# Four of six feature blocks of three batches transposed by DMA, in an mLSTM cell followed by a Fourier mix and an MLP

## The chip, the cores and the metric

The kernel runs on one core of one Trainium2 chip. The engines are TensorE (PE; its weight loads are PEld), VectorE (DVE), ScalarE (ACT), GpSimd (POOL) and SyncE (SP). SP computes nothing; it issues DMAs. The metric is the device time of one execution in microseconds (us). The runs shown before took 390.17, 390.27 and 390.72 us, with a median of 390.27.

## The reference

Two layers follow each other, over 4 batches, 8 heads, 768 tokens and head size 40 (so 320 features per token).

The first layer is an mLSTM cell: for each head a 40 x 40 state `C` and a vector `n` are carried over the tokens, with gates in a stabilised exponential form, and each token's output is `o * (C q) / max(|n q|, 1)`.

The second layer takes these outputs as `x` (4, 768, 320):

```
mixed = real(fft(fft(x, axis=tokens), axis=features))
u  = x + mixed
un = (u - mean(u)) / sqrt(var(u) + 1e-6)          # over the 320 features
out = u + max(un @ w_ch1, 0) @ w_ch2               # 320 -> 1280 -> 320
```

Everything is float32.

## The kernel before, in words

**Tiles.** A batch's 768 tokens are six chunks of 128 tokens. The mLSTM cell works chunk by chunk. The mix works on pairs of chunks, (0,5), (1,4) and (2,3), since the second of a pair is the mirror image of the first: one product over the features (`mix_feat`, L920) gives both chunks' mix in one PSUM bank `pu`. VectorE adds it to `x` (`mix_add`, L940: four additions and the statistics) and so makes `u` for one chunk. In this text one chunk's `u`, 128 tokens by 320 features, is called a feature block; there are six per batch, handled in the order `ORDER = (0, 5, 1, 4, 2, 3)`.

**From `u` to the MLP.** The MLP needs the features on the partitions, so each block is transposed. `mix_center` (L968) lets ACT subtract the mean and writes `uc`, 384 columns wide (320 features, 64 of them twice). `mix_turn` (L976) lets TensorE transpose it in three pieces of 128 x 128 into a PSUM bank `put`. `mix_turn_out` (L983) lets ACT copy that bank into `uT_bufs`. There are two `uT` buffers: the first holds blocks 0, 5 and 1, the second 4, 2 and 3; each is the moving operand of the MLP's first products (`mlp_in`, L1041, for the first batch; `mlp_block`, L1111, for the other three).

**The MLP.** For batches 1 to 3 both layers of the MLP are done with seven products in place of eight (a 2 x 2 block scheme). VectorE therefore forms sums: `weight_sums` and `out_weight_sums` once for the weights; `mlp_sums` (L1104) over the `uT` buffers at the beginning of a batch's MLP; `hidden_sums` (L1219) over the hidden layer, four sums S1 to S4 for each of three pairs of chunks. The second layer (`mlp_out_pair`, L1228) takes four steps per pair and adds its results to `u` by `residual` (L1186, the instruction is at L1190), and `store` (L1192) sends the chunk out. A PSUM bank of this layer is accumulated further after VectorE has read an intermediate value from it, so the next step of products waits for that reading.

**What sets the order.** All is written by hand. `at(slot, phase, fn, ...)` puts a call into a plan; `run` takes the plan in order of (slot, phase), and each engine gets its instructions in that order. Within a slot, the phases are EVAC (0), FILL (1), MAIN (2) and FILL_PE (3), with fractions between. A slot holds one step of the MLP in MAIN, and it is that which gives it its length, about 2.7 us where it is twenty products of 160 columns. The batches overlap: while batch b is in the second layer of its MLP, batch b+1 goes through its mix, and batch b+2 through its mLSTM cell. The MLP of batch b begins at slot `s_mlp` (31 + 32 b); its mix begins at `s_mix`, which is `s_mlp` - 9 for batch 1 and `s_mlp` - 12 for batches 2 and 3. `plan_batch` (L1312) holds the slots, counted from `s_mix`, of the three feature products (`feat`), of the six additions (`add`) and of the six centrings and transposes (`turn` and `late`).

**Queues.** All DMAs are issued by SP, in the order of the plan; a DMA that must wait holds up all behind it. SP's queue carries the loads of the mLSTM chunks (`mlstm_load`, `mlstm_load_max`, `mlstm_load_decay`, `mlstm_load_o`), moves of rows within SBUF (`halves_rows`) and the stores. ACT's queue carries the exponentials of the mLSTM chunks (L491) beside the centrings and copies.

**PSUM.** Four banks serve the mix and the MLP. Until batch 1 they are taken in the order of the string `turn` (L86), afterwards as the table `MIX` (L802) says.

The two buffers `hT_bufs` are used in batch 0 only.

Of the kernel before, what the change touches and what calls it, by code (L numbers as in the profile page):

```python
# [10 lines left out]
FP = mybir.dt.float32  # L11
BF = mybir.dt.bfloat16
I32 = mybir.dt.int32
U32 = mybir.dt.uint32
AF = mybir.ActivationFunctionType
# [4 lines left out]
L = 128  # L20
# [24 lines left out]
M_INIT = -1.0e30  # L45

# [7 lines left out]
def kernel(  # L54
# [31 lines left out]
    turn = iter("3210321032120312031230123012012301023130201320132013203120123021320321")  # L86
# [21 lines left out]
    uT_bufs = [const.tile([L, 3, TG, L], FP, name=f"uT{n}") for n in range(2)]  # L108
# [10 lines left out]
    G_d = dram.tile([NT, BH, L], FP, name="G_d")  # L119

# [641 lines left out]
    def plan_halves(b, s0, stride=3):  # L762
        for c in range(NT):
            s = s0 + stride * c
            t = 22 + 2 * c if b == 1 and c < 3 else s - 5
            at(t, FILL, mlstm_load, b, c)
# [13 lines left out]
            if (b, c) == (3, 2):  # L780
                at(s + 2, MAIN + 0.1, halves_weigh, b, c)
            else:
                at(s + 1, FILL + 0.55 if b == 1 and c > 0 else MAIN + 0.7, halves_weigh, b, c)
# [6 lines left out]
            at(s + (5 if (b, c) == (2, 2) else 4), {(2, 4): FILL + 0.3, (3, 3): FILL - 0.3}.get((b, c), FILL + 0.3 if b == 1 else MAIN + 0.55), mlstm_finish, b, c)  # L790
# [11 lines left out]
    MIX = {"z": (2, 3), "zt": 2, "u": (3, 2, 2), "ut": (3, 3, 3, 3, 2, 3)}  # L802
# [172 lines left out]

    def mix_turn(b, c):  # L976

        k = mixes[b]
        pt = k.pt[c] = bank("put", [L, 3, L], MIX["ut"][ORDER.index(c)] if b > 1 else None)
        for ch in range(3):  # L980
            nc.tensor.transpose(pt[:, ch, :], k.uc[c].rearrange("p two n -> p (two n)")[:, ch * L:(ch + 1) * L], ident)  # L981

    def mix_turn_out(b, c):  # L983
        k = mixes[b]
        n = ORDER.index(c)
        nc.scalar.copy(out=uT_bufs[n // TG][:, :, n % TG, :], in_=k.pt[c])  # L986
# [23 lines left out]
    def plan_mix(b, s0, x_done, s_feat, s_add, s_turn):  # L1010
        for j in range(TG):
            p = TG - 1 - j
            at(x_done[j] + (b > 1 and j == TG - 1), FILL + 0.5 if b < 2 else FILL_PE + 0.2, mix_fold, b, p)
            if b == 0:
                at((s0 - 4, s0 - 2, s0)[j], FILL_PE + 4, mix_seq, b, p, (0, 1))
                at((s0 - 2, s0 - 2, s0)[j], FILL_PE + 4, mix_tail, b, p)
            elif b == 1 or j == 0:
                if b > 1:
                    for step, slot in enumerate((x_done[0], x_done[-1] + 2, x_done[-1] + 6)):
                        at(slot, FILL_PE + 0.25, mix_fold_again, b, step)  # L1020
                at(s0, FILL_PE + 4, mix_seq, b, p, (0,))
                at(s0 + 1, FILL_PE + 4, mix_seq, b, p, (1,))
                at(s0 + 2, FILL_PE + 4, mix_tail, b, p)
        for i in range(2):
            at(s0 + 1 if b == 0 else s0 + 1 + i, FILL, mix_seq_out, b, i)
        at(s0 + (1 if b == 0 else 3), FILL + 0.1, mix_tail_out, b)
        for p in range(TG):
            at(s_feat[p], FILL_PE + 4, mix_feat, b, p)
        for c, a, t in zip(ORDER, s_add, s_turn):
            at(a, FILL if b < 2 else MAIN - 0.3 if c == 0 else MAIN + 0.5, mix_add, b, c)  # L1030
            at(t, FILL + 0.1, mix_center, b, c)
# [9 lines left out]
    def mlp_in(b, gr, f):  # L1041
# [3 lines left out]
        u = [uT_bufs[gr][:, ch].rearrange("p c t -> p (c t)") for ch in range(3)]  # L1045
# [55 lines left out]
    def mlp_u(gr, ch):  # L1101
        return uT_bufs[gr][:, ch].rearrange("p c t -> p (c t)")

    def mlp_sums(n0, n1):  # L1104

        T2, T3, T4 = w1x["T"]
# [164 lines left out]
    def plan_mlp(b, s):  # L1271
# [20 lines left out]
        for n in range(TG) if b > 0 else ():  # L1292
            for step in range(4):
                at(s, MAIN, mlp_out_pair, b, n, step)
                if n < TG - 1 and step > 1:
                    for j in (2 * step - 3, 2 * step - 2):
                        at(s, MAIN + 0.6, hidden_sums, n + 1, (j,))
# [14 lines left out]
    def plan_batch(b, s_mlstm, s_mix, s_mlp):  # L1312
# [9 lines left out]
        else:  # L1322
            feat = [s_mix + c for c in ((3, 4, 6) if b == 1 else (3, 4, 7))]
            add = [s_mix + c for c in ((4, 4, 5, 6, 7, 7), (4, 5, 5, 6, 8, 9), (4, 4, 5, 6, 8, 9))[b - 1]]
            turn = [s_mix + c for c in ((5, 6, 6) if b == 1 else (6, 7, 8))]
            late = [s_mix + c for c in ((7, 8, 8) if b == 1 else (9, 10, 10))]
# [165 lines left out]
```

## Time and profile before

| | before |
|---|---|
| median of the runs | 390.27 us (390.17 to 390.72) |
| profiled execution, its own time | 390.34 us |
| span of its trace | 388.6 us |
| granted TensorE clock | 1.00 |
| TensorE busy | 378.2 us, 97% |
| VectorE busy | 276.2 us, 71% |
| ACT busy | 172.4 us, 44% |
| POOL busy | 136.7 us, 35% |
| transposes of the mix (L981) | 72 |
| copies from `put` (L986) | 24, 477 ns each |
| centrings (L974) | 24, 613 ns each |

How to read it: the busy time of TensorE counts an instruction from its start to its modelled end, and neighbouring products overlap, so that the distance from one start to the next is shorter than the duration shown. In a list of waits, "A <- B: 0.6, 2, 0.3" says that A waited for B 0.6 us in total, twice, 0.3 us at the longest. In the chain that ended last, each row is a start, a length, and the engine and line that the end of the program is traced back to.

The mix and the change of batch from the trace, where the first product of the MLP starts: batch 1 at 161.6 us, batch 2 at 246.6 us, batch 3 at 324.0 us.

### The profile page before, as it was taken

Reading aid. Unit: us, or ns where it says so; the run is one execution under the profiler, and the core shown is the slowest. Engines: PE = TensorE matmul, PEld = TensorE weight load, DVE = VectorE, ACT = ScalarE, POOL = GpSimd, SP = SyncE. Lnnn points to the kernel's source line nnn. Section 1 sums busy time; section 2 is a strip of 40 time slices with the busy share of each in tenths; the row PEclk is TensorE's granted clock in tenths of the full one; section 3 lists DMA queues with packets and bytes.
Section 4 is the critical chain, followed back from the end, with each engine's and each line's share of the span. In section 5 each row is a group of like instructions: output and inputs, shape, how many; then the busy total and the mean of one; then the engine's idle time right before and its main releaser. Section 6 shows DMA issues by size and latency. Waiting matters only on the chain.

```text
span 388.6 us, 10587 instructions
## 1 busy us (share of the span) xinstructions
PE 378.2 (97%) x4174; PEld 276.4 (71%) x4174; DVE 276.2 (71%) x671; ACT 172.4 (44%) x481; POOL 136.7 (35%) x237
## 2 busy tenths in 40 slices
PE   8999899999999999999999999999999999999996
PEld 6887455556567677665579989755588995556996
DVE  8699987599698687576975699767655785246652
ACT  6996367377352124564462315454530133545000
POOL 5787415277955433172354133541500000020000
PEclk9999999999999999999999999999999999999999
DMA  7969499678494435538601636400000000000101
GB/s 213 313 195 306 134 236 249 185 217 232 143 229 131 126 98 156 147 87 221 143 11 36 156 101 185 126 19 2 0 2 34 18 19 34 2 0 0 35 34 35
DMA packets 25631, 44.78 MB, mean 115 GB/s; under 512 B 5727, under 2 KB 14766, under 8 KB 25454
## 3 DMA queue, kind: packets, MB, share of 16 engines
q1 hardware_dynamic: 25582, 44.11, 40.8%
q8 instruction: 33, 0.54, 0.6%
q14 instruction: 16, 0.13, 0.1%
HBM read 38.49 MB, written 4.12 MB: 110 GB/s over the span
## 4 chain that ended last, share of the span: by engine, by line
PE 79%; DVE 11%; ACT 4%; DMA 2%; issue 2%; POOL 1%; DVEq 0%; ACTq 0%; POOLq 0%
PE po L1240 20%; PE pm L1121 15%; PE po L1184 8%; PE pm L1059 7%; PE ph L519 4%; PE pm L1126 4%; PE pu L938 4%; PE ps L519 3%; DMA so<-in_o 2%; PE pm L1050 2%; PE put L981 2%; PE pz L907 1%; PE pz L895 1%; DVE h L1130 1%; PE pi L139 1%
## 5 line engine op out<-in xcount | busy, mean ns | idle before, releaser
L1190 DVE SCALAR_TENSOR_TENSOR x<-po,rstd,x 128x160 f32<-128x160 f32 (+1 forms) x69 | 27.1, 394 | 37.7 <-PE po L1240 32.5
L1130 DVE TENSOR_TENSOR h<-h,pm 128x384 f32<-128x384 f32 x60 | 30.5, 549 | 27.1 <-PE pm L1121 12.4
L652 POOL TENSOR_TENSOR C<-C,decB 128x164 f32<-128x164 f32 x30 | 15.9, 529 | 67.9 <-DVE C L667 43.2
L1121 PE MATMUL pm<-uT,w_sb 128*128 128x384 f32 x90 | 37.7, 506 | 1.3 <-DVE uT L1109 0.6
L491 ACT ACTIVATE W<-W,colT 128x64 f32<-128x64 f32 x144 | 37.5, 339 | 1.0 <-DMA W<-M_d 1.0
L1184 PE MATMUL po<-w_sb,h 128*128 128x320 f32 x120 | 34.2, 435 | 0.0
L1005 POOL TENSOR_TENSOR t<-rstd 128x6 f32<-128x6 f32 x12 | 3.3, 272 | 79.9 <-DVE v L999 79.4
L515 POOL TENSOR_SCALAR_AFFINE_SELECT W<-W 64x512 f32<-64x512 f32 x36 | 27.3, 758 | 10.8 <-ACT W L491 5.3
L1059 PE MATMUL pm<-uT,w_sb 128*128 128x384 f32 x80 | 29.2, 500 | 0.1
L1184 PEld LDWEIGHTS po<-w_sb,h 128*128 128x128 f32 x120 | 22.3, 190 | 9.5 <-issue 0.6
L501 POOL TENSOR_TENSOR qg<-qk,Gb 128x512 f32<-128x512 f32 (+1 forms) x21 | 27.1, 1292 | 2.8 <-DMA Gb<-G_d 2.8
L1240 PE MATMUL po<-T,S 128*128 128x160 f32 x180 | 27.8, 301 | 0.3 <-DVE x L1190 0.3
L1240 PEld LDWEIGHTS po<-T,S 128*128 128x128 f32 x180 | 25.5, 190 | 1.7 <-DVE x L1190 0.5
L1121 PEld LDWEIGHTS pm<-uT,w_sb 128*128 128x128 f32 x90 | 15.5, 189 | 15.6 <-DVE h L1130 6.7
L1240 PE MATMUL po<-w_sb,h 128*128 128x160 f32 x180 | 26.3, 300 | 0.0
L1240 PEld LDWEIGHTS po<-w_sb,h 128*128 128x128 f32 x180 | 25.2, 190 | 1.4 <-DVE x L1190 0.3
L986 ACT COPY uT<-put 128x384 f32<-128x384 f32 x24 | 11.2, 477 | 30.1 <-PE put L981 30.1
L507 POOL TENSOR_TENSOR vw<-kvt,colT 128x328 f32<-128x328 f32 x23 | 19.9, 863 | 12.7 <-DMA qk<-in_qkT 10.1
L1177 ACT ACTIVATE h<-h 128x384 f32<-128x384 f32 x45 | 23.1, 520 | 2.0 <-DVE h L1130 2.0
L1126 PE MATMUL pm<-uT,w1t_sb 64*128 64x384 f32 x120 | 23.4, 508 | 0.0
L1059 PEld LDWEIGHTS pm<-uT,w_sb 128*128 128x128 f32 x80 | 14.1, 189 | 9.6 <-issue 1.9
L974 ACT ACTIVATE uc<-x 128x384 f32<-128x384 f32 x24 | 14.4, 613 | 12.6 <-DVE x L966 11.1
(241 smaller groups left out, 841.5 us busy)
## 6 DMA issues: line engine op xcount, KB each, us to landing
kvt<-in_kv SPq DMA_DIRECT2D x24, 336.0 KB
qk<-in_qkT SPq DMA_DIRECT2D x48, 160.0 KB
raw<-in_w SPq DMA_DIRECT2D x10, 640.0 KB
Gb<-G_d SPq DMA_DIRECT2D x36, 128.0 KB
W<-M_d SPq DMA_DIRECT2D x36, 128.0 KB
so<-in_o SPq DMA_DIRECT2D x24, 160.0 KB
out<-x SPq DMA_DIRECT2D x24, 160.0 KB
x<-so SPq DMA_DIRECT2D x9, 140.0 KB
```

What stands on the lines that cost most here:

```text
L491: nc.scalar.activation(out=k.W[:, h, :], in_=M, func=AF.Exp, scale=-1.0, bias=colT[:, c, 0, b * H + h:b * H + h + 1])
L501: nc.gpsimd.tensor_tensor(out=k.qg[:, :, t], in0=k.qk[:, 0, :, t], in1=k.Gb[:, :, t], op=OP.mult)
L515: nc.gpsimd.affine_select(out=W, in_=W, compare_op=OP.is_ge, fill=0.0, base=base, pattern=[[0, H], [step, LH]], channel_multiplier=-1)
L519: nc.tensor.matmul(out, w, x, start=start, stop=True, skip_group_check=True)
L1059: nc.tensor.matmul(k.pm[i], w1_sb[:, ch, f0:f0 + L], u[2 * ch], start=(ch == 0 and not ahead), stop=(ch == 1 and ahead), skip_group_check= ...
L1121: nc.tensor.matmul(bank, w, u, start=start, stop=True, skip_group_check=True)
L1126: nc.tensor.matmul(bank, block(w1t_sb, i)[rows], mlp_u(gr, 1)[rows], start=False, stop=True, skip_group_check=True)
L1130: nc.vector.tensor_tensor(out=h, in0=h, in1=bank, op=OP.add)
L1177: nc.scalar.activation(out=h, in_=h, func=AF.Relu, scale=-1.0)
L1184: nc.tensor.matmul(k.po[gr, i], hidden(gr, f)[:, i * L:(i + 1) * L], w2_sb[:, f, :], start=(f == 0), stop=(f == NFF - 1))
L1190: nc.vector.scalar_tensor_tensor(out=u, in0=po, scalar=k.rstd[:, c:c + 1], in1=u, op0=OP.mult, op1=OP.add)
L1240: nc.tensor.matmul(po, a[:, f], w[:, f], start=start and f == 0, stop=f == half - 1, skip_group_check=True)
```

## The change

For batches 1, 2 and 3, the first four blocks in `ORDER` (0, 5, 1 and 4; `TURNED = 4`) no longer go through TensorE, the PSUM bank `put` and the copy by ACT. After the centring, `mix_words` lets ACT copy the block as halfwords: each float32 of `uc` is two words of 16 bits, and the copy puts the 384 first words of a token and then its 384 second words into one of the buffers `hT_bufs`. ACT itself issues a DMA that writes this to a scratch tensor in HBM, 256 rows (token and word) of 384 halfwords. `mix_words_turn` lets SP issue a transposing DMA from there into `uT`, where the 256 halfwords of a feature are again 128 float32 values. Blocks 2 and 3, and all of batch 0, are transposed as before.

The layout of `uT` changes with it, from (3, chunk, 128) to (chunk, 3, 128): a block is now one contiguous piece, and the MLP reads three pieces of 128 columns.

Around this, places in the plan change: the second product over the tokens and the tail of batches 2 and 3 one slot earlier; the feature products and additions of the first four blocks one slot earlier in part, some centrings too; in batch 2's stretch (the MLP of batch 1) S3 and S4 of the last pair later or at another phase; three placements of the mLSTM chunks of batch 3 (`halves_weigh` of chunk 1, `mlstm_finish` of chunk 0, and the load of chunk 5 two slots earlier); the PSUM banks of the third feature product.

```diff
-    turn = iter("3210321032120312031230123012012301023130201320132013203120123021320321")
+    turn = iter("321032103212031203123012301201230102313020132013201320312012302130")
...
-    uT_bufs = [const.tile([L, 3, TG, L], FP, name=f"uT{n}") for n in range(2)]
+    uT_bufs = [const.tile([L, TG, 3, L], FP, name=f"uT{n}") for n in range(2)]
...
+    uc_d = dram.tile([B - 1, TURNED, 2 * L, 3 * L], U16, name="uc_d")
...
-            at(t, FILL, mlstm_load, b, c)
+            at(*((t - 2, FILL + 0.95) if (b, c) == (3, 5) else (t, FILL)), mlstm_load, b, c)
...
+            elif (b, c) == (3, 1):
+                at(s + 2, MAIN + 0.4, halves_weigh, b, c)
...
-    MIX = {"z": (2, 3), "zt": 2, "u": (3, 2, 2), "ut": (3, 3, 3, 3, 2, 3)}
+    MIX = {"z": (2, 3), "zt": 2, "u": (3, 2, 3), "ut": (3, 3, 3, 3, 2, 3)}
...
+    def mix_words(b, c):
+        k = mixes[b]
+        n = ORDER.index(c)
+        words = hT_bufs[n % 2].rearrange("p n t -> p (n t)").bitcast(U16)[:, 0:6 * L].rearrange("p (w m) -> p w m", w=2)
+        of = k.uc[c].rearrange("p two n -> p (two n)").bitcast(U16).rearrange("p (n w) -> p w n", w=2)
+        nc.scalar.copy(out=words, in_=of)
+        nc.scalar.dma_start(out=uc_d[b - 1, n].rearrange("(t w) m -> t w m", w=2), in_=words)
+
+    def mix_words_turn(b, c):
+        n = ORDER.index(c)
+        nc.sync.dma_start_transpose(out=uT_bufs[n // TG][:, n % TG].bitcast(U16), in_=uc_d[b - 1, n])
...
-        nc.scalar.copy(out=uT_bufs[n // TG][:, :, n % TG, :], in_=k.pt[c])
+        nc.scalar.copy(out=uT_bufs[n // TG][:, n % TG], in_=k.pt[c])
...
-                at(s0 + 1, FILL_PE + 4, mix_seq, b, p, (1,))
-                at(s0 + 2, FILL_PE + 4, mix_tail, b, p)
+                at(s0 + (b == 1), FILL_PE + 4, mix_seq, b, p, (1,))
+                at(s0 + (2 if b == 1 else 1), FILL_PE + 4, mix_tail, b, p)
...
+            if b > 0 and c in ORDER[:TURNED]:
+                at(t, FILL + 0.1, mix_center, b, c)
+                at(t, FILL + 0.11, mix_words, b, c)
+                at(*{(1, 1): (t, FILL + 0.95), (1, 4): (t, FILL + 0.95), (2, 5): (t + 1, FILL + 0.95),
+                     (2, 1): (t + 2, FILL - 0.7), (2, 4): (t + 1, FILL - 0.7)}.get((b, c), (t + 1, FILL - 0.55)),
+                   mix_words_turn, b, c)
+                continue
...
-        return uT_bufs[gr][:, ch].rearrange("p c t -> p (c t)")
+        return uT_bufs[gr][:, :, ch]
...
-                        at(s, MAIN + 0.6, hidden_sums, n + 1, (j,))
+                        at(*((s, MAIN + 0.6) if b != 1 or n == 0 or j < 3 else (s + j - 3, MAIN + 0.2)), hidden_sums, n + 1, (j,))
...
-            feat = [s_mix + c for c in ((3, 4, 6) if b == 1 else (3, 4, 7))]
-            add = [s_mix + c for c in ((4, 4, 5, 6, 7, 7), (4, 5, 5, 6, 8, 9), (4, 4, 5, 6, 8, 9))[b - 1]]
-            turn = [s_mix + c for c in ((5, 6, 6) if b == 1 else (6, 7, 8))]
-            late = [s_mix + c for c in ((7, 8, 8) if b == 1 else (9, 10, 10))]
+            feat = [s_mix + c for c in ((3, 4, 5) if b == 1 else (2, 3, 7))]
+            add = [s_mix + c for c in ((4, 4, 5, 5, 6, 6), (3, 4, 5, 6, 8, 9), (3, 4, 5, 6, 8, 9))[b - 1]]
+            turn = [s_mix + c for c in ((5, 5, 6) if b == 1 else (5, 6, 7))]
+            late = [s_mix + c for c in ((6, 7, 8) if b == 1 else (8, 10, 10))]
```

## The prediction

> **What bounds the kernel.** The page first: the span, TensorE's share of it, and the chain that ended last.
>
> ```profile
> span 388.6 us, 10587 instructions
> PE 378.2 (97%) x4174; PEld 276.4 (71%) x4174; DVE 276.2 (71%) x671; ACT 172.4 (44%) x481; POOL 136.7 (35%) x237
> ...
> PE 79%; DVE 11%; ACT 4%; DMA 2%; issue 2%; POOL 1%; DVEq 0%; ACTq 0%; POOLq 0%
> ```
>
> TensorE is busy for 97% of the span, so what leaves its queue shortens the kernel, unless something makes it wait. Next, TensorE's waits from 120 to 330 us, the stretch that holds all three changed stages:
>
> ```profile
> PE pm L1121 <- DVE uT L1109: 0.6, 2, 0.3
> PE pm L1121 <- DVE h L1130: 0.5, 2, 0.3
> PE po L1240 <- DVE x L1190: 0.3, 1, 0.3
> PE ph L519 <- ACT warm L699: 0.3, 1, 0.3
> ```
>
> Total, count, longest: 1.7 us of waiting in 210 us. Are the transposes in that queue paid in full? Their group (all 72), then TensorE's timeline in batch 3 (start, length):
>
> ```profile
> L981 PE MATMUL put<-ident,uc x72: 272/273/332, 54.0 to 322.5; 128*128 128x128 f32 x72
> ```
>
> ```profile
> 312.83 2.88 PE L1240 MATMUL po<-w_sb,h 128*128 128x160 f32 x20
> 315.55 0.49 PE L981 MATMUL put<-ident,uc 128*128 128x128 f32 x3
> 315.88 1.52 PE L1240 MATMUL po<-T,S 128*128 128x160 f32 x10
> 317.24 1.52 PE L1240 MATMUL po<-w_sb,S 128*128 128x160 f32 x10
> ```
>
> One transpose lasts 273 ns, but they overlap: what counts is from the first start to the next product's, 315.88 - 315.55 = 0.33 us for a block's three. Last, the chain in batch 2, where it leaves TensorE:
>
> ```profile
> 224.72 0.39 DVE x L1190
> 225.10 0.23 DVE x L960
> ...
> 235.35 0.73 DVE s_last L1226
> 236.08 0.24 DVE C L667
> 236.32 0.30 DVE x L1190
> 236.62 0.04 issue
> 236.67 0.40 PE po L1240
> ```
>
> From 224.7 to 236.6 VectorE works without a gap of its own, and TensorE's product at 236.67 waits for a residual that stands at the end of this backlog. In batch 2, then, VectorE is as tight as TensorE; in batches 1 and 3 it has holes.
>
> **The skill.** (1) "DMA: Bandwidth & Descriptors", section DMA Transpose (X-bar): it transposes two-byte elements only, is issued from SP or ACT, and must write to SBUF. Hence float32 is split into two halfwords. No run before shows one. (2) The same page, Latency and other measured facts: 261 GB/s in one kernel, 350 to 400 for a contiguous one; not in this trace. (3) "VectorE: DVE Perf Modes", The three transpose paths: 1309 ns for one 128x128 two-byte tile through DMA, 390 ns on TensorE; the trace has 273 ns (float32) and 0.11 us of queue. (4) "ScalarE: Activation LUTs", What ACT_TABLE_LOAD costs: an activation with immediate scale takes 186 ns + 0.833 ns per element. That gives 506 ns for 384 elements; the trace has 477 for L986, so it agrees roughly.
>
> **The change, part by part.**
>
> *Removed from TensorE:* four blocks in each of three batches, three transposes each. 12 x 0.33 = 3.96 us. Some intervals are longer (0.38 at 229.21, 0.39 at 232.77), but those follow small products, and the cold start passes to whatever comes next, so I take 0.33. From ACT go 12 copies of 477 ns.
>
> *Added to ACT, per block:* a copy of 768 halfwords, read at a stride of two. Estimate by (4): 186 + 640 = 826 ns; if the stride costs double, 1.5 us. Then one DMA issue; ACT issues none before, and SP's for a store take 349 ns. Net 0.83 + 0.35 - 0.48 = 0.7 us per block, 8.4 us in all (up to 16). ACT has 13.8 of 38.9 us busy from 122.8 to 161.7, 17.3 of 46.8 in batch 2, 8.4 of 39.2 in batch 3: its idle time covers this. Behind it in ACT's queue stand the exponentials of the next chunk; their masks and weighing come a slot or more (2.7 us) later. Without that cover it would be up to 1.4 us per slot.
>
> *Added to DMA, per block:* 196 KB written to HBM and read back turned. The last store is issued at 385.9 and the span ends at 388.6, so at most 2.7 us for 160 KB; I take 2.5 for the write. The transposing read: at best as a plain DMA, 2.5 us; at worst six 128x128 tiles of 1.31 us one after another, 7.9 us. I take 3.
>
> *Is it in time?* Batch 1 is tightest. Its adds and centres run in slots 58 to 60; ACT gets blocks 1 and 4 at about 147.9 (before's clock), needs per block 0.62 + 0.83 + 0.35 = 1.8, and has issued block 4's write at 151.5. It lands at 154, is turned by 157. TensorE wants it when the MLP begins: 161.7 - 1.3 = 160.4, with sums (L1109) just after. Slack 3.4 us. In batch 2 blocks 1 and 4 are turned in slot 92, from about 237 to 240.5, due at 246.6 less three or four blocks and the wait, 244.8: slack about 4. In batch 3 block 4's copy is done at about 314, written by 316.5, turned by 319.5, due at 324.0 - 1.3 = 322.7: slack 3.
>
> *SP's queue:* each transpose waits for its write, and everything behind it waits too. Between them in batch 1 stand the loads of chunk (2,4), used four slots later; in batch 2, the loads of (3,4) and (3,5), the latter placed two slots earlier, ahead of the waits. Stores need no haste. The loads wait up to 2 to 4 us more and are used at least 8 us later: nothing. If that cover went, POOL's query scaling would start late and products from chunks wait, some 2 us once.
>
> *Moved products* (second sequence product, tail, features, one slot earlier): the same instructions, at no cost. The tail's copy (0.48) still lies under the 2.72 us of ten-plus-ten products between it and the features. New PSUM banks for the third feature block: its old content is added two slots before.
>
> *VectorE in batch 2:* the add of block 5 (1.75 us, 224.99 to 226.76 in the trace) leaves the backlog for a slot with holes of 1.1 us, and S4 (0.73) goes behind the residual. That residual comes 2.5 us earlier, TensorE only three blocks (1.0 us) earlier, so the wait of 0.30 and the cold start after it (2.98 against 2.72) go: 0.5 us. The waits at 249.9 and 255.0 follow from VectorE's sums at 247.8 to 254, whose order does not change: 0.
>
> *uT read in three pieces:* TensorE reads it as 3 x 128 columns with gaps, in 360 instructions. An operand read at a stride of two costs no more than a contiguous one (L895: two of 193 columns from 203.97 to 204.31, 0.34 us; L904: 122.02 to 122.35, 0.33), so I take 0; the upper end is the difference, 5 ns on each, 1.8 us.
>
> **Sum** against the profiled execution's 390.34 (span 388.6 and 1.7 around it): 390.34 - 3.96 - 0.5 = 385.9. The median of the runs is 390.27, 0.07 less: 385.8.
>
> **Rivals.**
>
> *The transposes are slow (slower than before).* If one holds the crossbar for T and they run in series, batch 1's four start at about 146.8, when SP has issued the row moves that it begins at 144.65 (2.10 us), and end at 146.8 + 4T, against 160.4. Beyond T = 3.4 TensorE stands still at the start of the MLP, where nothing else is in its queue. With T = 4.5 batch 1 loses 4.4 us, all of the gain: there it decides. With T = 5: 6.4 in batch 1, and in batch 2 two transposes from 237 to 247 against 244.8, 2.2 more: 385.8 + 8.6 = 394.4. At 7.9: 18, 8 and about 2, some 414. For it: four are issued nearly together, and the price per tile in (3). Against: that price is for one tile alone, with its latency; the rates in (2) move 196 KB in 0.5 to 0.75 us.
>
> *VectorE keeps batch 2 (less gain).* If the backlog of 224.7 to 236.6 only moves, batch 2's 1.3 and 0.5 are lost, or ACT's and SP's added work brings as much waiting anywhere: 387.6. For it: VectorE's closed chain. Against: the holes of 1.1 us in the slots to which the add goes.
>
> *More gain.* VectorE, relieved, also begins the sums of batch 2 earlier, and the 0.6 us of waits there and the lost starts behind them go: 384.6. Against: they hang on a residual that TensorE itself releases at 244.75.
>
> *No change:* the transposes were hidden anyway, or waits take exactly their time. Against: each product starts right after them, with no idle time shown.
>
> **Chances.** Forecast 0.60, its own range 385.1 to 386.8; less gain 0.15 (386.8 to 389.4); more gain 0.06 (384.5 to 385.1); no change 0.04; slow transposes 0.15. A measurement here tells about 0.2% (0.8 us) from nothing, so faster 0.81, same 0.04, slower 0.15. The three gaining cases hold 0.81: the range is 384.5 to 389.4, whose upper end also takes in 1.8 us for the three pieces and more.
>
> **What would show it.** 36 transposes on TensorE in place of 72, at the same 273 ns; TensorE's busy time down by some 4 us and its waits before the first product of each MLP under 0.5 us. ACT with 12 new copies near 0.83 us. On SP, transposes whose waits are under 4 us; no late loads in POOL's waits. In batch 2 no wait of TensorE for L1190. I am wrong if TensorE waits for uT (L1109 or L1121) by microseconds, if the copies take over 1.5 us and the exponentials come late, or if products from uT get slower than the 0.341 us of 14 in 4.78.

## The result, and the profile after

| | before | after |
|---|---|---|
| median of the runs made together | 390.74 us | 387.6 us |
| ratio after / before, 95% interval | | 0.9922 [0.9906, 0.9938] |
| profiled execution | 390.34 us | 387.23 us |
| its span | 388.6 us | 385.4 us |
| TensorE busy | 378.2 us | 374.8 us |

The kernel became faster by 0.78%, some 3.0 us. The forecast was 4.5 us. Measured again (experiment 5) the ratio was 0.9932 [0.9916, 0.9948]. Both intervals lie above the ratio that the forecast implies, 385.8 / 390.27 = 0.9885: the direction and the main mechanism were right, about 1.4 us of the gain did not come. The median of 387.6 us lies in the range that the forecast gave to "less gain" (386.8 to 389.4, chance 0.15) and not in its own (385.1 to 386.8, chance 0.60).

The page of the changed kernel: span, busy times, the DMA queues that carry most and that carry instructions (packets, MB, share of 16 engines), and the chain.

```profile
span 385.4 us, 10538 instructions
PE 374.8 (97%) x4138; PEld 273.4 (71%) x4138; DVE 277.5 (72%) x671; ACT 177.5 (46%) x481; POOL 138.0 (36%) x237
...
q1 hardware_dynamic: 35182, 46.47, 45.0%
...
q8 instruction: 32, 0.52, 0.6%
...
PE 82%; DVE 9%; ACT 3%; DMA 2%; issue 2%; POOL 1%; DVEq 0%; SPq 0%; POOLq 0%; ACTq 0%
```

TensorE still bounds the kernel at 97% of a shorter span; its share of the chain rose from 79 to 82%. The parts of the change, by their tiles (count, then shortest, median and longest duration in ns):

```profile
L998 PE MATMUL put<-ident,uc x36: 272/273/330, 54.1 to 319.3; 128*128 128x128 f32 x36
L986 ACT COPY h<-uc x12: 815/832/833, 143.6 to 309.7; 128x768 uint16<-128x768 uint16 x12
L987 ACTq DMA_DIRECT2D uc_d<-h x12: 338/338/577, 144.4 to 310.5; - x12
L991 SPq DMA_TRANSPOSE uT<-uc_d x12: 1209/1240/2201, 147.0 to 313.5; - x12
```

Half of the 72 transposes are left on TensorE. The copy of 768 halfwords takes 832 ns, where the estimate was 826. The issue of a transposing DMA holds SP for 1.24 us; I had counted SP's time only as waiting. Now TensorE's waits from 120 to 330 us (total, count, longest), as before shown for the kernel before:

```profile
PE ph L522 <- issue: 0.9, 1, 0.9
PE put L998 <- ACT uc L979: 0.4, 1, 0.4
PE po L1264 <- DVE x L1214: 0.3, 1, 0.3
PE pm L1145 <- DVE uT L1133: 0.2, 1, 0.2
PE ph L522 <- ACT warm L702: 0.2, 1, 0.2
PE pm L1145 <- DVE h L1154: 0.2, 1, 0.2
```

Three of these are new, and they are where the missing gain must be looked for first: a stop of 0.9 us at products from a chunk that waited for nothing the profile shows, a transpose (`put`) that waits for its centring, and a product that waits for a residual at a new place. TensorE's timeline says where (start, length, and in brackets the idle time before it):

```profile
221.02 1.63 PE L1264 MATMUL po<-T,S 128*128 128x160 f32 x10 [0.34 <-DVE x L1214]
248.47 0.44 PE L522 MATMUL ph<-kvt,W 64*64 64x41 f32 x16 [0.92 <-issue]
319.07 0.55 PE L998 MATMUL put<-ident,uc 128*128 128x128 f32 x3 [0.39 <-ACT uc L979]
```

The same timeline, read from start to start of TensorE's instructions, gives the length of each stretch. "Mix" runs from the first sequence product of batch 1, or from the first product of the previous MLP's second layer, to the first product of this batch's MLP; "first layer" from there to the second layer; the last column ends where the last run of ten products starts.

| us | mix 1 | first layer 1 | mix 2 | first layer 2 | mix 3 | MLP 3 to last products |
|---|---|---|---|---|---|---|
| before | 39.61 | 38.01 | 46.93 | 38.09 | 39.33 | 59.93 |
| after | 38.39 | 37.77 | 46.08 | 38.04 | 38.33 | 59.92 |
| difference | -1.22 | -0.24 | -0.85 | -0.05 | -1.00 | -0.01 |
| forecast | -1.32 | 0 | -1.82 | 0 | -1.32 | 0 |

The differences add up to -3.37 us; with 0.18 us of a later start they make the -3.19 us by which the last products start earlier. The forecast's terms add up to -4.46 us. So 1.1 us is missing in this pair of traces: 0.97 in batch 2, 0.32 in batch 3 and 0.10 in batch 1, less 0.30 gained where nothing was forecast.

### The profile page after: what moved, and what is told of

Read it like the earlier page. It is cut to its first block, busy times and chain, and to the rows that moved or that the text cites. A ratio compares the mean times of both kernels' runs of the same rounds, so it can differ in the third digit from the quotient of the medians.

```text
span 385.4 us, 10538 instructions
## 1 busy us (share of the span) xinstructions
PE 374.8 (97%) x4138; PEld 273.4 (71%) x4138; DVE 277.5 (72%) x671; ACT 177.5 (46%) x481; POOL 138.0 (36%) x237
## 4 chain that ended last, share of the span: by engine, by line
PE 82%; DVE 9%; ACT 3%; DMA 2%; issue 2%; POOL 1%; DVEq 0%; SPq 0%; POOLq 0%; ACTq 0%
PE po L1264 21%; PE pm L1145 16%; PE po L1208 9%; PE pm L1083 7%; PE ph L522 5%; PE pm L1150 4%; PE pu L943 4%; PE ps L522 4%; DMA so<-in_o 2%; PE pm L1074 2%; PE pz L912 1%; PE pz L900 1%; PE put L998 1%; DVE h L1154 1%; PE pi L142 1%
## 5 line engine op out<-in xcount | busy, mean ns | idle before, releaser
L494 ACT ACTIVATE W<-W,colT 128x64 f32<-128x64 f32 x144 | 37.4, 338 | 1.3 <-ACT h L986 0.5
L1250 DVE TENSOR_TENSOR S<-h,h 128x640 f32<-128x640 f32 (+2 forms) x24 | 17.1, 710 | 3.5 <-ACT h L1201 3.5
```

What stands on the lines that cost most here:

```text
L494: nc.scalar.activation(out=k.W[:, h, :], in_=M, func=AF.Exp, scale=-1.0, bias=colT[:, c, 0, b * H + h:b * H + h + 1])
```

## The experiments

Twelve kernels ran. Ratios are to the kernel before on the same chip. Each kernel has one trace. In six traces of kernels that are the same up to the MLP of batch 2, mix 2 lies between 46.08 and 46.95 us; the table of the changed kernel above is the lowest of them.

**1. Without the route.** The transposes of the four blocks are gone and nothing takes their place: no copy to halfwords, no write, no transposing read, so that `uT` holds old values in these blocks.

```diff
-                at(t, FILL + 0.11, mix_words, b, c)
-                at(*{(1, 1): (t, FILL + 0.95), ...}.get((b, c), (t + 1, FILL - 0.55)), mix_words_turn, b, c)
```

> The changed kernel without the copy into halfwords, the write to HBM and the transposing DMA of blocks 0, 5, 1 and 4; the MLP of batches 1 to 3 then reads what lies in uT from earlier (this part of the computation is left out). Theory A: the whole DMA route lies beside other work, and the 1.3 us that the forecast is short of comes from waits for VectorE and ACT in batches 2 and 3. Then this kernel takes as long as the changed one, 387.2 to 387.7 us, with the same waits of TensorE: 0.3 us for a residual near 221 us, 0.4 us for a centring near 319 us. Theory B: the route costs something (SP's queue, DMA traffic, ACT's longer queue, a stop of instructions such as the 0.92 us near 247.5). Then this kernel is 0.8 to 1.3 us faster, 386.0 to 386.6, and the 0.92 us stop is gone.

Measured: 386.93 against 391.26 us, ratio 0.9889 [0.9871, 0.9908], span 385.2. The removal together with the new plan is worth 4.3 us. The interval, 3.6 to 5.0 us, holds the forecast's 4.46 and also the 3.96 of the transposes alone. Its stretches: 38.38, 37.65, 45.80, 38.10, 38.39, 59.93; they add up to 3.65 us less than before. TensorE's waits in the same window:

```profile
PE pm L1141 <- DVE uT L1129: 0.6, 2, 0.3
PE pm L1141 <- DVE h L1150: 0.5, 2, 0.3
PE put L998 <- ACT uc L979: 0.4, 1, 0.4
PE po L1260 <- DVE x L1210: 0.3, 1, 0.3
PE ph L522 <- ACT warm L702: 0.3, 1, 0.3
```

The waits for the residual (0.34 us at 220.98) and for the centring stay without the route: they belong to the rearranged plan. The stop named "issue" is gone: that belongs to the route. So in the single traces the route costs 0.2 us. In the timed runs it is 0.33% (0.9922 against 0.9889) or 0.43% (0.9932 in experiment 5), 1.3 to 1.7 us; these are ratios from separate measurements (0.9932 on another chip), each to the kernel before of its own, and the intervals just meet in the first case and do not in the second. I take it that the route costs about that over many executions, more than in the trace shown; the six traces compared below bear this out.

**2. The rearrangement alone.** All transposes on TensorE (`if False:` in place of `if b > 0 and c in ORDER[:TURNED]:`), batch 1 as before and the PSUM banks of the transposes fitted to it; batches 2 and 3 in the new order.

```diff
-            if b > 0 and c in ORDER[:TURNED]:
+            if False:
-            add = [s_mix + c for c in ((4, 4, 5, 5, 6, 6), (3, 4, 5, 6, 8, 9), (3, 4, 5, 6, 8, 9))[b - 1]]
+            add = [s_mix + c for c in ((4, 4, 5, 6, 7, 7), (3, 4, 5, 6, 8, 9), (3, 4, 5, 6, 8, 9))[b - 1]]
```

> Only the plan of batches 2 and 3 is rearranged as in the changed kernel; all six blocks are transposed on TensorE (batch 1 as in the kernel before, PSUM banks of the transposes fitted to it). Theory A: the rearrangement by itself is worth little, within 0.5 us of the kernel before (390.3 to 391.2), since what it takes off VectorE's backlog at 236 us it gives back at 221 us; the gain is that of the removed transposes. Theory B: the rearrangement makes half of the gain or more: 389.2 us or less.

Measured: 392.08 us, ratio 1.001 [0.9991, 1.0029]; mix 2 takes 47.02, mix 3 39.62 us. The rearrangement gives nothing by itself that this measurement can tell. The 0.5 us that I had put down to VectorE's relief in batch 2 are not there: the wait for the residual is 0.34 us, at 222.56 us where it had been 0.30 at 236.67. And in batch 3 the last transpose waits for its centring here too, though all transposes are on TensorE:

```profile
323.02 0.55 PE L998 MATMUL put<-ident,uc 128*128 128x128 f32 x3 [0.44 <-ACT uc L979]
```

**3. The finish moved back.** `mlstm_finish` of chunk 0 of batch 3 stands ahead of the residual in the changed plan; here it has its old phase.

```diff
-{(2, 4): FILL + 0.3, (3, 3): FILL - 0.3, (3, 0): FILL - 0.1}
+{(2, 4): FILL + 0.3, (3, 3): FILL - 0.3}
```

> The changed kernel with one placement undone: the five VectorE instructions that finish chunk 0 of batch 3 stand behind the two residuals of their slot again, not in front of them. Theory A: they (1.75 us with a slow L719 among them) are what makes TensorE wait for the residual near 221 us. Then that wait (0.34 us, 0.5 us with the cold start) is gone, and the span shrinks by 0.4 to 0.6 us against the changed kernel's 385.4. Rival: the addition of block 0, moved one slot earlier, fills VectorE by itself; then the wait stays within 0.2 us of what it was, or moves to the next residual near 224 or 234 us, and the span does not change.

Measured: 389.57 us, ratio 0.9962 [0.9943, 0.998]. The wait at 221 is gone, so the finish does make it; but my theory that it therefore costs time falls. The waits:

```profile
PE ph L522 <- issue: 2.0, 1, 2.0
PE po L1264 <- DVE x L1214: 1.6, 1, 1.6
```

A wait for a residual came back later and longer, 1.6 us at 224.85 in place of 0.34 at 221.02: the finish now runs from 222.57 to 224.27, behind an addition (220.90 to 222.65) and ahead of the next residual. The forecast called the place "a slot with holes of 1.1 us"; addition and finish together need 3.4, and the finish in front is the better of the two orders.

**4. A late transpose, to measure one.** The read of block 4 of batch 3 is issued only when it is due.

```diff
-(2, 4): (t + 1, FILL - 0.7)}
+(2, 4): (t + 1, FILL - 0.7), (3, 4): (t + 3, MAIN + 0.9)}
```

> The changed kernel with the transposing DMA of block 4 of batch 3 issued only after the first store of slot 126, near 321 us, so that the MLP has to wait for it and the wait's end shows when it lands. If a transposing DMA needs 2.5 to 3.5 us from the beginning of its issue to its use, VectorE's first sum of the MLP of batch 3 (L1133) starts at 323.5 to 325 us, and the span grows by 2 to 3.5 us. If it needs 7.9 us (six tiles one after another), the sum starts near 329 us and the span grows by 7 to 8 us.

Measured: 393.68 us in one run, span 391.8. The issue in SP's timeline of its trace:

```profile
323.07 1.21 SPq L991 DMA_TRANSPOSE uT<-uc_d  x1
```

The instruction that waits for it, in VectorE's timeline of the same trace:

```profile
326.20 0.56 DVE L1133 TENSOR_TENSOR e<-uT 128x384 f32<-128x384 f32 x1 [3.58 <-DMA uT<-uc_d]
```

From the start of the issue to the first use it takes 326.20 - 323.07 = 3.13 us, of which 1.21 is the issue. I had taken 3. The price of one tile in the Trainium skill ("VectorE: DVE Perf Modes", The three transpose paths), 1309 ns, does not add up over the six tiles of one DMA: 7.9 us is excluded here, and with it the rival of the slow transposes.

**5. The changed kernel again**, with no edit, on another chip than experiments 1 to 4.

> The changed kernel as it is, timed beside the next three on one chip. The same gain as on record, 0.99 to 0.994 of the kernel before.

Measured: 388.57 against 391.11 us, ratio 0.9932 [0.9916, 0.9948]. In its trace mix 2 takes 46.63 us, 0.55 more than in the first one, and two waits stand out:

```profile
PE ph L522 <- issue: 1.2, 1, 1.2
PE po L1264 <- DVE den L717: 0.6, 1, 0.6
```

The stop is at the same instruction as before. The second wait names VectorE's `den`, but what the product needs, the residual, had ended at 243.84 us, and the product starts at 244.64: 0.8 us in which it waited for something other than the residual. Both are taken up below.

**6. Batch 2's old order, with the DMA route.** Additions, feature products, tail, S3 and S4, finish, load of chunk 5 and banks of batch 2's stretch as before the change; routes kept, the reads in the slot after the centring.

```diff
-            add = [s_mix + c for c in ((4, 4, 5, 5, 6, 6), (3, 4, 5, 6, 8, 9), (3, 4, 5, 6, 8, 9))[b - 1]]
-            late = [s_mix + c for c in ((6, 7, 8) if b == 1 else (8, 10, 10))]
+            add = [s_mix + c for c in ((4, 4, 5, 5, 6, 6), (4, 5, 5, 6, 8, 9), (3, 4, 5, 6, 8, 9))[b - 1]]
+            late = [s_mix + c for c in ((6, 7, 8), (9, 10, 10), (8, 10, 10))[b - 1]]
```

> The changed kernel with batch 2's part of the plan as in the kernel before: its sequence products, tail, features, additions and centrings, the sums S3 and S4, the two placements and the load of batch 3's chunks, and the PSUM bank of the third feature product; the four blocks still go by DMA. Theory A (the rearrangement of batch 2 gives nothing, VectorE's work decides there): the stretch from the beginning of the second layer to the first product of batch 2's MLP, 46.93 us before and 46.08 after, is 45.9 to 46.3 us, and the span that of the changed kernel within 0.4 us. Theory B (the forecast: the rearrangement is worth 0.5 us): 46.4 to 46.9 us with TensorE's wait for a residual near 235 us back and longer than 0.3 us, and the span 0.4 to 0.9 us longer. Theory C (the rearrangement is needed so that the DMAs land in time): TensorE or VectorE waits for uT by a microsecond or more at the beginning of batch 2's MLP.

Measured: 390.91 us, ratio 0.9994 [0.9968, 1.0021], with `po` waiting 1.2 us for the residual and a stop of 1.5 us. There is no wait of microseconds for `uT`, so the route is in time even in the old order. Mix 2 takes 46.65 us, against 45.80 in experiment 1: both without the gap of experiment 5, so the old order costs 0.85 us there, as much as the residual's wait grew (1.2 against 0.34). So the rearrangement, worth nothing alone, pays once the transposes are gone from TensorE: with TensorE's slots shorter and VectorE's work the same, the old order makes the residual late. In the timed runs it is worth 0.6% (0.9994 against 0.9932), 2.3 us, which is more than this wait. The trace is of the shortest execution, 388.71 us. In 8 of the 14 executions the granted clock was 0.996 or lower, against 5 of 22 in experiment 5; the medians of the others are 389.6 and 388.1, 1.5 us apart. What makes up the rest of that was not traced.

**7. The third feature product one slot earlier** in batch 3, to take the wait for the last centring away.

```diff
-(2, 3, 7))]
+(2, 3, 7 if b == 2 else 6))]
-(3, 4, 5, 6, 8, 9))[b - 1]]
+(3, 4, 5, 6, 7, 8))[b - 1]]
-(8, 10, 10))]
+(8, 10, 10) if b == 2 else (8, 9, 10))]
```

> The changed kernel with one thing moved: in batch 3 the third feature product, the additions of blocks 2 and 3 and block 2's centring stand one slot earlier. Theory A: in batch 3 the chain residual, addition, centring, last transpose bounds the end of the mix, so that block 4's 0.33 us, removed from between, came back as a wait (0.39 us for a centring near 319 us, 0.55 us with the cold start). Then that wait is gone and the stretch from the second layer's beginning to the MLP of batch 3 falls from 38.33 to 37.8 us, the span by 0.5 us. Theory B: VectorE has no room a slot earlier either; the wait moves to a residual or to the first sums, and the stretch stays within 0.15 us.

Measured: 389.72 us, ratio 0.9966 [0.9948, 0.9984]. The wait for the centring is gone, but mix 3 grew from 38.33 to 39.39 us, because a residual in batch 3 is now late; I put this down to the additions that stand ahead of it. The waits of `po` in this window, of which 1.4 us is in batch 3:

```profile
PE po L1264 <- DVE x L1214: 1.8, 2, 1.4
```

VectorE is the tighter one here; moving its work forward in this way costs more than the 0.4 us.

**8. The same, with the first two sums of batch 3's MLP earlier**, ahead of the last residual.

```diff
-            at(s_mlp, EVAC + 0.5, mlp_sums, 0, 3 if b == 2 else 4)
+            if b == 3:
+                at(s_mlp - 1, MAIN - 0.05, mlp_sums, 0, 2)
+            at(s_mlp, EVAC + 0.5, mlp_sums, 2 if b == 3 else 0, 3 if b == 2 else 4)
```

> The kernel of the run before with one thing more: the first two of the MLP's sums of batch 3 stand on VectorE in front of the last residual of the second layer, not behind it. Then TensorE's wait of 0.24 us for these sums (0.34 us with what goes before it) goes too, and the kernel is 0.8 to 0.9 us faster than the changed one in the span. If the last residual, now later, holds up a bank instead, nothing is gained over the run before.

Measured: 388.79 us, ratio 0.9944 [0.9923, 0.9966]; mix 3 stays at 39.38, the last segment falls from 59.94 to 59.42 us. So the sums are worth 0.5 us there, while the 0.8 to 0.9 us against the changed kernel that I expected did not come.

**9. Two reads left out.** The reads of blocks 1 and 4 of batch 2, issued one after the other at 237.6 us, are gone (these two blocks of `uT` keep old values); copies and writes stay.

```diff
+                if (b, c) not in ((2, 1), (2, 4)):
```

> The changed kernel without the transposing reads of blocks 1 and 4 of batch 2 (the two issued one after the other at 237.6 us); their copies by ACT and writes to HBM stay, and uT keeps old values in these two blocks. Theory A (these two reads, close together and followed by loads, hold the transfers that the beginning of batch 2's MLP needs): the stop of TensorE named issue at the first chunk products after the MLP begins (247 to 250 us, 0.9 to 2.0 us in every trace with the route) is gone, the sums of VectorE come no later, batch 2's stretch and the 38 us after its MLP's start fall to 45.8 and 38.1 us, and the ratio to the kernel before falls from 0.992 by 0.002 to 0.004, to about 0.989. Theory B (the cost lies in the writes and copies, or is spread over all twelve reads): the stop stays, and the ratio gains at most a sixth of 0.0035, 0.0006.

Measured: 387.76 against 391.1 us, ratio 0.9901 [0.9865, 0.9937], from six runs: too wide to decide by time. In the trace mix 2 takes 45.79 and the first layer 38.21 us, as theory A says, and the product before batch 2's MLP starts without the gap of experiment 5. But a stop of 0.7 us at `ph` is still there. In this one trace theory A holds for the gap and not for the stop.

**10. Plain reads in place of transposing ones**, with the same bytes at the same places (`uT` gets blocks that are not turned; the copy by ACT leaves the words in their order).

```diff
-        nc.sync.dma_start_transpose(out=uT_bufs[n // TG][:, n % TG].bitcast(U16), in_=uc_d[b - 1, n])
+        nc.sync.dma_start(out=uT_bufs[n // TG][:, n % TG].rearrange("p c t -> p (c t)").bitcast(U16),
+                          in_=uc_d[b - 1, n].rearrange("(t w) m -> t (w m)", w=2))
```

> The changed kernel with the same copies, the same writes and reads of the same bytes at the same places, but with a plain read from HBM in place of the transposing one, so that uT gets blocks that are not turned. Theory A (the transposing form is what costs: it keeps SP for 1.24 us at its issue and the DMA engines for some 1.35 us of all 16): SP's issue falls to about 0.35 us, the busy share of the DMA engines from 240 to 242 us falls below 1, the stop named issue is gone, and the ratio is that of the kernel without the route, 0.989. Theory B (any traffic of this size at these places costs the same, or the waits of SP for the writes do): ratio 0.992 as in the changed kernel, and the stop stays.

Measured: 387.66 us, ratio 0.9912 [0.9887, 0.9938]; the interval holds both theories' ratios. In the trace the issue takes 0.39 us on SP (median of 12) instead of 1.24, and the gap before batch 2's MLP is gone (mix 2: 45.79). But a stop of 1.8 us stands at `ph`. The load of the DMA engines differs as expected; this is the main queue's line (packets, MB, share of 16 engines) in two microseconds after the two reads, of the changed kernel from 240 to 242 us:

```profile
q1 hardware_dynamic: 530, 0.24, 142.4%
```

And with plain reads in the same two microseconds, since their issue ends at 240.00 there and at 240.14 in the changed kernel:

```profile
q1 hardware_dynamic: 235, 0.55, 96.1%
```

With the transposing reads the packets, counted together, took more time than 16 engines have in the stretch (they overlap) and moved 0.24 MB; with plain ones they moved 0.55. The transposing form costs SP and the engines more, and yet the stop does not need it.

**11. Each read issued twice.**

```diff
+        for _ in range(2):
+            nc.sync.dma_start_transpose(out=uT_bufs[n // TG][:, n % TG].bitcast(U16), in_=uc_d[b - 1, n])
```

> The changed kernel with each transposing read issued twice, the second with the same source and destination. It takes SP's queue another 1.24 us per block, 15 us in all, and the DMA engines some 1.35 us more per block. Theory A (the route's cost of about 1.3 us comes from the reads' load on SP and the DMA engines): the ratio rises from 0.992 by 0.003 to 0.006, the stop at batch 2's MLP grows beyond 2 us, and in batch 1 the later reads stay within the slack (landing about 2.5 us later, against a slack of 3.4). Theory B (the slacks are as large as the forecast said, and the cost is not in the reads): ratio 0.992, with no new wait. Rival C: a read and its repetition run one after the other beyond the slack of batch 2 or 3, and TensorE or VectorE waits for uT by more than 1 us.

Measured: 416.78 us, ratio 1.0647 [1.0608, 1.0685]. None of the sizes was foreseen, since the repetition writes the same place and so waits on SP for the first to land. The chain that ended last, in batch 1 (start, length, what):

```profile
153.82 3.09 DMA uT<-uc_d
156.91 0.02 issue
156.92 1.21 SPq L992
```

TensorE's waits from 120 to 350 us:

```profile
PE pm L1146 <- DMA uT<-uc_d: 17.7, 2, 9.1
PE pm L1146 <- DVE uT L1134: 2.0, 1, 2.0
```

So this did not double a load; it set reads in series, 3.09 + 1.2 = 4.3 us for this pair. It shows the mechanism that the forecast's rival described, transposes in series that TensorE waits for at the start of the MLP: 17.7 us of waits for `uT`, in a kernel that is 25.7 us slower than before. It also measures the read twelve times, since a block's second issue starts when the first has landed: 2.9 to 3.2 us after it for eight blocks, and 4.6 to 5.8 for the other four. So the 3.1 us of experiment 4 is not a fixed duration. As a test of what the load costs this kernel is void.

**12. The early sums alone**, on the changed kernel: experiment 8's edit of `mlp_sums` without that of experiment 7.

> The changed kernel with one edit: the first two of the four sums of batch 3's MLP go one slot earlier on VectorE, ahead of the last residual of batch 2. In an experiment before, together with another edit, the last segment fell from 59.93 to 59.42 us. Theory A (the sums do this alone): last segment 59.4 us, ratio to the kernel before 0.991, that is 0.0013 below the changed kernel's. Theory B (they push the residual that TensorE waits for, and batch 3's stretch grows by as much): ratio 0.992 to 0.993.

Measured: 387.59 against 391.1 us, ratio 0.9907 [0.9875, 0.9939]. Mix 3 stays at 38.35 and the last segment falls to 59.39 us: the mechanism is as theory A says, 0.53 us. The ratio agrees with it and is the lowest of the kernels that leave nothing out, but its interval holds the changed kernel's 0.9922 too, so in time it is not told apart.

## The stop that has no releaser

In every trace with a part of the route, but for experiment 11, TensorE stops at the same instruction, products from a chunk some 4 us into batch 2's MLP, for 0.6 to 2.0 us; in none without it (before, experiments 1 and 2). In experiment 11 it has just stood still for 9.06 us at the start of that MLP. The profile calls it "issue". In some of the traces a second gap lies 5 to 7 us before the stop, at `po`, the last product before that MLP. One queue helps: q8, which carries instructions, 16 KB in one packet at a time, 32 in the whole span. Here is its line in the quarter of a microsecond from 245.75 in the changed kernel:

```profile
q8 instruction: 1, 0.02, 23.6%
```

And in the quarter from 242.75 in the kernel without the route (experiment 1):

```profile
q8 instruction: 1, 0.02, 23.0%
```

Narrowed down to 0.05 us, packet and end of TensorE's gap stand thus in six of the traces:

| kernel | packet | gap ends at | distance |
|---|---|---|---|
| after, gap before `po` | 240.50 | 242.98 | 2.48 |
| 5, gap before `po` | 242.00 | 244.64 | 2.64 |
| 12, gap before `po` | 241.50 | 243.93 | 2.43 |
| after, stop at `ph` | 245.95 | 248.47 | 2.52 |
| 3, stop at `ph` | 247.90 | 250.42 | 2.52 |
| 5, stop at `ph` | 247.95 | 250.40 | 2.45 |
| 9, stop at `ph` | 248.60 | 250.97 | 2.37 |
| 10, stop at `ph` | 248.60 | 251.03 | 2.43 |
| 12, stop at `ph` | 246.35 | 249.12 | 2.77 |

The gap ends 2.4 to 2.8 us after a packet of instructions, wherever the packet falls; in experiments 4, 6, 7 and 8 it is 2.3 to 2.7. In the kernel without the route the packets come at 238.65 and 242.95, four microseconds ahead of the same two places (the load of `po`'s weights at 242.64, and `ph` at 247.03), and there is no gap. In experiments 9 and 10, where no gap is shown before `po`, the packet came 2.87 and 2.34 us ahead of that load.

The two places are also the same distance apart in the program. From the end of the gap to the end of the stop, here in the changed kernel (stretch and its length, then busy time and count of PE, PEld, DVE, ACT and POOL, granted clock, DMA share, GB/s), TensorE has 126 products and 126 weight loads:

```profile
242.98:248.46 5.48, 4.57 (x126) 3.63 (x126) 5.23 (x10) 3.33 (x13) 3.94 (x7) 1.00 0.81 236
```

With the four semaphore instructions that the trace records among them these are 256 instructions, and experiments 5, 7 and 12 have the same 126 and 126. The whole program has 8276 products and loads for its 32 packets, 259 to a packet, and the kernel before 8348 for 33, 253. So the packets fit TensorE's instructions, 256 at a time, and gap and stop then lie at the beginnings of two successive packets. The reading that fits all this: TensorE comes to the end of one packet before the next has arrived. Whose the packets are no view says; the count and the constant distance speak for it. That the data transfers hold the packets up is inferred: from 236 to 248 us the DMA engines' share is 0.95 in the changed kernel, 0.45 without the route (experiment 1). Why no other packet comes too late stays open, and no experiment has the writes or ACT's copies without the reads.

Gap and mix 2 can be compared in six traces whose plan is the same up to there. The gap is taken before the load of `po`'s weights:

| kernel | gap | mix 2 | mix 2 less the gap |
|---|---|---|---|
| 1, 9 and 10 | none | 45.80, 45.79, 45.79 | |
| after | 0.27 | 46.08 | 45.81 |
| 8 | 0.51 | 46.33 | 45.82 |
| 5 | 0.81 | 46.63 | 45.82 |
| 7 | 1.00 | 46.82 | 45.82 |
| 4 | 1.00 | 46.83 | 45.83 |
| 12 | 1.13 | 46.95 | 45.82 |

All that mix 2 has over the kernel without the route is this gap, 0.9 us in the middle of the six. The first trace of the changed kernel, on which the table of the result rests, has the smallest. Mix 2 and the first layer of batch 2 together take 0.2, 0.8, 1.0, 1.1, 1.1 and 3.1 us more in the six than in experiment 1, most of what the timed runs lose by the route.

What the stop costs is less than its length: it lets VectorE's sums catch up, so that the waits for `uT` and `h` of the kernel without the route (0.34 at 247.79, 0.31 at 252.90) shrink or vanish. With a stop of 0.62, 0.68, 0.92, 0.99 (twice) and 1.19 us the first layer of batch 2 takes 37.74, 38.21, 38.04, 38.13, 38.11 and 38.33 us, against 38.10 without one. With 1.53, 1.77 and 2.03 it takes 39.01, 38.90 and 39.50. About the first microsecond is nearly free.

Experiment 8 is apart: after a stop of 2.05 us its first layer takes 40.66. There the granted clock is 0.55 from 252.4 to 256.2 us:

```profile
252.40:256.20 3.80, 3.80 (x9) 1.62 (x7) 3.10 (x8) 1.44 (x5) 1.16 (x2) 0.55 0.17 47
```

So it is in experiment 4 after its wait for the late read (0.58 from 327 to 331), and in experiment 11 around its two long waits (0.50 from 166 to 179 and from 262 to 271), but not in experiment 3 after 2.03 us. In experiment 8 the first layer is 2.56 us longer than without a stop, more than the stop itself.

## Why the prediction was right, and where it was off

*The bound and the 0.33 us of a block: right.* Four blocks off the queue took 1.22 us from mix 1 (experiment 1: 1.23), where 1.32 was worked out. The removal with the new plan is worth 3.65 us in the traces and 4.3 in timed runs.

*VectorE in batch 2, 0.5 us: wrong.* This is the step "that residual comes 2.5 us earlier ... so the wait of 0.30 and the cold start after it go". The wait only moved, to 221.02 us, 0.34 long. (The cold start's 2.98 is 2.91 in the trace, 236.67 to 239.58; the term stays near 0.5.) I followed the addition out of the backlog and did not work out the slot it went to. The new order was not worthless: without it the removal would have lost 0.85 us to this wait (experiment 6). The chain there shows what comes together:

```profile
217.44 0.82 DVE s_last L1250
...
219.12 1.04 DVE so L719
220.16 0.02 issue
220.18 0.49 DVE so L723
220.67 0.30 DVE x L1214
220.97 0.04 issue
221.02 5.70 PE po L1264 x40
```

S4 and the finish stand ahead of the residual. The finish's L719 takes 1.03 us here and 0.49 in experiment 3, where it runs later; here GpSimd's `vw` product runs from 219.06, there no GpSimd instruction runs beside it. That half microsecond is more than the wait. Whether it comes from the two engines working at once was not tried.

*Batch 3: a third of a microsecond too much.* Nothing was to be lost there. The last `put` waits 0.39 us for its centring (319.07). Before, the transposes of block 4 (318.60) lay between the product that a residual waits for and this put, and covered part of the addition and centring of the last block. In experiment 2 they are still on TensorE, but one slot earlier (316.33), and the put waits 0.44 us. So it is the missing cover that costs: the new plan would have taken it away even without the DMA route. The forecast asked this question of ACT's and VectorE's moved work, and not of what the transposes themselves had hidden. Experiment 7 shows that the obvious cure costs 1.06 us.

*First layer of batch 1: 0.24 us of gain not foreseen.* Its first six products took 2.40 us to the next start before and take 2.04. Experiment 1 has the gain too, experiment 2 does not; its cause is open.

*ACT's copy and issue: right.* 832 + 338 ns; from 120 to 330 us GpSimd waits 1.0 us for an exponential (W, L494), where it waited 3.3 before.

*The write and the read: right.* SP waited for writes 4.0 us in three waits, 2.8 at the longest; the bound named was "under 4 us" each. The read takes 3.13 us in experiment 4 where 3 was taken, though up to 5.8 in experiment 11, and in the window from 120 to 330 us neither TensorE nor VectorE waits for a DMA into `uT` in the changed kernel.

*"The loads wait up to 2 to 4 us more ...: nothing": the term that was mis-sized.* TensorE and VectorE do not wait for these loads, true, and GpSimd for one of them only once, 1.1 us. But I priced the new traffic only by who waits for its data. The route costs 1.3 to 1.7 us between the timed runs of experiment 1 and of the changed kernel, and the traces show one place at which it does, the two gaps of TensorE around the start of batch 2's MLP, in which no data was awaited. Against experiment 1, mix 2 alone is longer by 0.28 us in the first trace of the changed kernel, by 0.83 in the second, and by up to 1.15 in the others of the same plan. The term was put at 0 without a bound for this.

*`uT` in three pieces: right.* The last segment is 59.93 us before and 59.92 after, with 120 products that read it.

*The rivals.* Slow transposes: excluded by 3.13 us, and shown as a mechanism by experiment 11. "VectorE keeps batch 2", at 387.6 us, gave the measured median to the digit; that much is luck, but it came nearer than the forecast. The 0.5 is lost. Of batch 2's whole gain 1.13 us is left without the route, and 0.85 down to nothing in the six traces with it. What takes it is not VectorE's chain alone but, in the rival's own second half, waiting that comes with the added work, by the reading above for TensorE's instructions. More gain and no change: no. Of the signs that the forecast named, two failed: in batch 2 a product does wait for the residual, and the gap before that batch's MLP, for which under 0.5 us was named, is 0.8 us or more in four of the six traces.

## What to carry to other kernels

Work that is moved off the bounding engine, or to another place in its queue, is worth its interval there, but ask what it covered: the chain that ran under it (here addition, centring, put) comes into the open. A reordering that is worth nothing alone can be what makes the removal pay, so judge the two together (mix 2 before, with the new order alone, with the route and the old order, with the new order and neither transposes nor route: 46.93, 47.02, 46.65, 45.80 us). And price added DMA traffic also where no instruction waits for its data: an idle stretch with no releaser, at the same instruction in every trace, is worth comparing with the queue that carries instructions. Take more than one trace of a kernel before a difference of half a microsecond is believed.

## What the hardware showed beyond what was expected

A transposing DMA of 256 rows of 384 halfwords holds the issuing SP for 1.24 us, against 0.39 for a plain one of the same bytes, and is usable 3.1 us after its issue began, or up to 5.8 us after it in experiment 11. TensorE's gaps end 2.3 to 2.8 us after a 16 KB packet on the instruction queue; gap and stop lie 256 of TensorE's instructions apart. Without the route the packets come 4.0 to 4.1 us ahead of the same two places. After a stop of 2.05 us the granted clock was 0.55 for nearly four microseconds (experiment 8); after one of 2.03 it stayed at 1.00 (experiment 3).
